# Stores moved to ScalarE's queue, four staging tiles and smaller weight-sum stores in a two-half SwiGLU feed-forward

## The chip, the cores and the metric

The kernel runs on one core of one Trainium2 chip. The metric is device microseconds of one execution; the time of a kernel is the median of its runs. Engines are named as in the profile: PE (TensorE; PEld is its weight load), DVE (VectorE), ACT (ScalarE), POOL (GpSimd) and SP (SyncE, which here only issues DMAs). ACT, too, has a DMA queue of its own.

## The reference

A transformer block in fp32 on x of 2048 x 576: a modulation from `c`, a layer norm, attention with a compressive memory in 4 segments and 32 heads of 18, a residual, a second layer norm, and a SwiGLU feed-forward with a hidden size of 4608, with a residual. The change touches the feed-forward alone:

```python
def _B_ref(x, w_gate, w_up, w_down):
    g = _silu(x @ w_gate)
    u = x @ w_up
    return (g * u) @ w_down
...
h = _layernorm(x, axis=-1) * (1 + cb) + sb
x = x + gb * _B_ref(h, B_w_gate, B_w_up, B_w_down)
```

## The kernel before, in words

The first 640 us are modulation, projections and attention. Then the feed-forward runs in two halves of 1024 tokens (`t` = 0 and 1), each a loop over 18 pairs `p` of hidden blocks (256 hidden columns). In each pair the gate product (z = 0) and the up product (z = 1) are formed as a 2 x 2 x 2 block product with seven products instead of eight (a Strassen scheme): a tile `O` of seven operands for the weights, a tile `y` of seven operands for the activations, and fixed sums of the products. A pair is therefore 14 steps `k`, one product each: seven matmuls of 512 columns (L1148), since each fp32 operand is split in a high and a low part: ACT casts the high part (`wh`, L1112), DVE subtracts for the low part (`wl`, L1113). `order` gives the sequence of the products. Casts run six steps ahead in the first half, five in the second.

`O` has 7 slots of [3][128] fp32 a partition: two full blocks of 128 contraction rows and a third block that holds the remainder of 32 rows four times. Four slots are loaded from HBM (`load_o`, L1081, 768 KB); three more and a replacement of the fourth are sums of them, made by POOL in four instructions (`sum_o`, L1103), so four slots (0, 4, 5, 6) hold sums. Only `prep_r` reads the third block; it makes the tile `wr` of the remainder (ACT cast L1097, DVE subtract L1098). In the first half the sums are stored to HBM (`store_o`: two DMAs to `oD`, 192 and 576 KB, all three blocks of the four slots), as is `wr` (`store_r` to `rD`, 336 KB), and the sums of the down-projection weights (`wdD`, 1008 KB, L1465). The second half reads all three back (L1083 to L1085, L1094, L1122) and does no sums. `O` has two buffers, so the load of the next tile waits until the last `wl` of the tile two back is done.

All of this is an order written out by hand (`manual_schedule`). What a step issues stands in the loop from L1412 on. The steps of a first-half pair that matter here, before the change:

- step 0 and 1: `mul_d`, two multiplies on POOL of the down-projection weights `RW` by a modulation row; steps 2, 3, 8 and 7: `sum_d`, their sums on POOL; steps 4, 5, 6 and 10: `prep_d`, ACT casts of the slots of `RW` and DVE subtractions.
- step 1: `load_o` of the next pair's z = 0, then the stores of this pair's z = 1 sums and z = 0 `wr`. Step 7: the store of the z = 1 `wr`. Step 8: `load_o` of the next pair's z = 1. Step 9: the store of `RW`, and the cast of the next pair's z = 0 remainder. Step 11: the store of the next pair's z = 0 sums. Step 12: the load of the next `RW`, a single buffer.
- steps 4 to 11: the down product of the previous pair, `plain`, 12 matmuls of 288 columns in each (L1288), added to `acc` by DVE (L1292).
- steps 1 to 10, in pairs after the first: one stage each of the generator `prep2`, which makes the second half's activation operands. It first normalizes five row blocks (load `ha` L1017, statistics L1024, store L1030), then for six pieces loads `xb` (L1040, L1043), transposes it on PE (L1048), evacuates it into `ha` (L1050) and makes seven operands. Each operand takes two stages: an ACT cast into a staging tile `st` (L1004), then a DVE subtraction (L1008 or L1011) and a store to `yD` (L1009 or L1012).

All these loads and stores are issued by SP, one after the other: a DMA whose wait isn't over holds up all that stand behind it. `st` has one buffer, so a cast into it waits until the store before has landed. The last first-half pair loads the seven operands `y` of the second half as their buffers come free (`load_y`), and with them the first `O` tiles and `wr` of the second half.

Of the kernel before, what the change touches and what calls it, by code (L numbers as in the profile page):

```python
# [7 lines left out]
F32 = mybir.dt.float32  # L8
F32R = mybir.dt.float32r
BF16 = mybir.dt.bfloat16  # L10
AF = mybir.ActivationFunctionType
ALU = mybir.AluOpType
# [3 lines left out]
P = 128  # L16
# [8 lines left out]
NF = FF // P  # L25
# [45 lines left out]
def f32(ap):  # L71
    return ap.bitcast(F32)
# [3 lines left out]
def block(ctx: ExitStack, tc: tile.TileContext, x, wqk, wv, wo, beta, wgu, wd, c, w_mod, out):  # L76
    nc = tc.nc
# [28 lines left out]
    dr = pool(ctx, "dr", space=DRAM)  # L106
# [42 lines left out]
    xD = [dr.tile([P, 4, D], F32, tag=f"xD{s}", name=f"xD{s}") for s in range(NSEG)]  # L149

    wdD = [dr.tile([P, 7, 288], F32, tag=f"wd{p}", name=f"wd{p}") for p in range(NF // 2)]
    oD = [[dr.tile([P, 4, 3, P], F32, tag=f"oD{p}_{z}", name=f"oD{p}_{z}") for z in range(2)] for p in range(NF // 2)]

    rD = [[dr.tile([96, 7, P], F32, tag=f"rD{p}_{z}", name=f"rD{p}_{z}") for z in range(2)] for p in range(NF // 2)]

# [92 lines left out]
    with ExitStack() as p1:  # L248
# [78 lines left out]
        with ExitStack() as p0:  # L327
# [27 lines left out]
            for p in (1, 0):  # L355
                for k in range(6):
                    for h in range(2):
                        r = 64 * (1 - p) + 32 * h
                        w = wm[p, k // 2][:, k % 2, 256:576] if h else wm[p, k // 2][:, k % 2, 0:256]
# [147 lines left out]
        for s in range(NSEG):  # L507
# [13 lines left out]
            for t in QKORD:  # L521
                if s == 0 and t + 3 < 9:
                    load_qk(t + 3)
                f = proj(s, t)
# [134 lines left out]
    op = pool(p2r, "op", side="right")  # L659
# [235 lines left out]
    NPR = NF // 2  # L895
# [10 lines left out]
            return ZML if p == NPR - 1 else ZM  # L906
        return ZM1 if p else ZMB

    SLOT = {1: 1, 2: 2, 3: 6, 4: 3, 5: 4, 6: 5, 7: 0}
    ACT_OP = {1: 0, 2: 1, 3: 2, 4: 6, 5: 3, 6: 4, 7: 5}  # L910

    def t_prep():
# [83 lines left out]
    def prep2():  # L996
        ha = xp.tile([P, 2, L], F32, tag="xs", name="ha")
        xb = xp.tile([P, 4, 2, P], F32, tag="xs", name="xb")[:, :, 0]
        t3 = x2p.tile([P, 256], F32, tag="t3", name="t3")

        def opr(kb, hv, o, f):
            n = P if kb < 2 else 96
            st = x2p.tile([P, 2, 256], F32R, tag="st", name="st")
            nc.scalar.copy(st[:n, 0], f)  # L1004
            c = slice(256 * hv, 256 * hv + 256)
            yield
            if kb < 2:
                nc.vector.tensor_tensor(st[:, 1], f, f32(st[:, 0]), op=ALU.subtract)  # L1008
                nc.sync.dma_start(yD[o][:, kb:kb + 3:2, c], f32(st))  # L1009
            else:  # L1010
                nc.vector.tensor_tensor(st[64:96, 0], f[64:96], f32(st[64:96, 0]), op=ALU.subtract)  # L1011
                nc.sync.dma_start(yD[o][:96, 4, c], f32(st[:96, 0]))  # L1012
            yield

        xl = ha.rearrange("p a b -> p (a b)")[:, :D]
        for sn, i in ((2, 3), (3, 0), (3, 1), (3, 2), (3, 3)):
            nc.sync.dma_start(xl, xD[sn][:, i, :])  # L1017
            for _ in range(3):
                yield
            st = x2p.tile([P, 2, 6], F32, tag="st3", name="st3")  # L1020
            mv = x2p.tile([P, 2], F32, tag="mv", name="mv")
            rs = x2p.tile([P, 1], F32, tag="rs", name="rs")
            for h in range(2):
                nc.vector.bn_stats(st[:, h, :], xl[:, 288 * h:288 * h + 288])  # L1024
            nc.vector.bn_aggr(mv, st)
            nc.vector.tensor_scalar(rs, mv[:, 1:2], EPS, None, op0=ALU.add)
            nc.gpsimd.tensor_tensor(rs, rs, mhalf[:, :1], op=ALU.pow)
            yield
            nc.vector.tensor_scalar(xl, xl, mv[:, 0:1], rs[:, 0:1], op0=ALU.subtract, op1=ALU.mult)
            nc.sync.dma_start(xhD[sn][:, i, :], xl)  # L1030
            yield
        for kb in range(3):
            n = P if kb < 2 else 96
            for hv in range(2):
                for kh in range(2):
                    c0 = 288 * kh + 128 * kb
                    for b in range(2):
                        src = xhD[2 + b][:, 2 * hv:2 * hv + 2, c0:c0 + min(P, 288 - 128 * kb)]
                        if kb < 2:
                            nc.sync.dma_start(xb[:, 2 * b:2 * b + 2, :], src)  # L1040
                        else:
                            for j in range(3):
                                nc.sync.dma_start(xb[:, 2 * b:2 * b + 2, 32 * j:32 * j + 32], src)  # L1043
                    for _ in range(3):
                        yield
                    pt = ps.tile([P, 4, P], F32, tag="M", name="pt", bufs=4)
                    for i in range(4):
                        nc.tensor.transpose(pt[:n, i, :], xb[:, i, :n], ident)  # L1048
                    c = 3 * kh + kb
                    nc.scalar.activation(ha[:n, kh], pt[:n].rearrange("p a b -> p (a b)"), AF.Identity,  # L1050
                                         scale=colm[:n, c, 0:1], bias=colm[:n, c, 1:2])
                    yield
                h00, h10, h01, h11 = [ha[:n, k, 256 * b:256 * b + 256] for k in range(2) for b in range(2)]
                nc.gpsimd.tensor_tensor(t3[:n], h11, h10, op=ALU.subtract)
                yield from opr(kb, hv, 0, h00)
                nc.gpsimd.tensor_tensor(h10, h10, h00, op=ALU.subtract)
                yield from opr(kb, hv, 5, t3[:n])
                yield from opr(kb, hv, 2, h11)
                yield from opr(kb, hv, 3, h10)
                nc.gpsimd.tensor_tensor(h11, h11, h10, op=ALU.subtract)  # L1060
                yield from opr(kb, hv, 1, h01)
                yield from opr(kb, hv, 4, h11)
                nc.gpsimd.tensor_tensor(h01, h01, h11, op=ALU.subtract)
                yield
                yield from opr(kb, hv, 6, h01)
# [5 lines left out]
    O, W, R, RW, DP = {}, {}, {}, {}, {}  # L1071
# [6 lines left out]
    def load_o(t, p, z):  # L1078
        O[p, z] = o = opl.tile([P, 7, 3, P], F32, tag="O", name="O", bufs=2)
        if t == 0:  # L1080
            nc.sync.dma_start(o[:, 0:4], wgu[p, z])  # L1081
        else:
            nc.sync.dma_start(o[:, 1:4], wgu[p, z][:, 1:4])  # L1083
            nc.sync.dma_start(o[:, 0], oD[p][z][:, 0])
            nc.sync.dma_start(o[:, 4:7], oD[p][z][:, 1:4])  # L1085

    def store_o(p, z):
        nc.sync.dma_start(oD[p][z][:, 0], O[p, z][:, 0])
        nc.sync.dma_start(oD[p][z][:, 1:4], O[p, z][:, 4:7])

    def prep_r(t, p, z):
        R[z] = r = wrp.tile([P, 7, P], F32R, tag="wr", name="wr")
# [6 lines left out]

    def sum_o(p, z, j):  # L1100
        o = O[p, z]
        d, a, b, op = ((4, 0, 3, ALU.add), (5, 4, 1, ALU.subtract), (0, 1, 0, ALU.subtract), (6, 2, 5, ALU.subtract))[j]
        nc.gpsimd.tensor_tensor(o[:, d], o[:, a], o[:, b], op=op)  # L1103

    def store_r(p, z):
        nc.sync.dma_start(rD[p][z], f32(R[z][0:96]))

    def prep_w(p, z, m):
        o = O[p, z][:, SLOT[m], 0:2]
# [14 lines left out]
    def mul_d(p, f):  # L1124
        v = RW[p][:, 2 * f:2 * f + 2].rearrange("p a b -> p (a b)")
        nc.gpsimd.tensor_tensor(v, v, gbB, op=ALU.mult)

    def sum_d(p, j):
        r = RW[p]
        d, a, b = ((4, 1, 0), (5, 3, 4), (6, 2, 5), (1, 3, 1))[j]  # L1130
        nc.gpsimd.tensor_tensor(r[:, d], r[:, a], r[:, b], op=ALU.subtract)
# [109 lines left out]
    NS = [7] * (NPR - 2) + [4] * 2  # L1241
# [65 lines left out]
    with tc.manual_schedule():  # L1307
# [51 lines left out]
        for i in range(4):  # L1359
            for h in range(2):  # L1360
                for c in range(WC):
# [8 lines left out]
                    if n in SS:  # L1370
                        j = SS.index(n)
# [22 lines left out]
        x2p = pool(p6, "x2p")  # L1394
# [17 lines left out]
        for p in range(NPR):  # L1412
# [4 lines left out]
            for k in range(14):  # L1417
                z, m = order(0, p)[k]
# [18 lines left out]
                else:  # L1437
# [5 lines left out]
                        prep_r(0, p, 1)  # L1443
                    elif k == 9:
                        prep_r(0, nx, 0)
                if k < 2:
                    mul_d(p, k)
                elif k in (2, 3, 8, 7) and p < NPR - 2:
                    sum_d(p, (2, 3, 8, 7).index(k))
                if not end and 4 <= k < 8:  # L1450
                    sum_o(nx, 0, k - 4)
                elif not end and 9 <= k < 13:
# [1 line left out]
                if k in (4, 5, 6, 10):  # L1454
                    j = (4, 5, 6, 10).index(k)
                    prep_d(p, (j // 2, j % 2), j)
                if k == 0 and p == 0:
                    store_o(p, 0)
                elif k == 1:
                    store_o(p, 1)  # L1460
                    store_r(p, 0)
                elif k == 7:
                    store_r(p, 1)
                elif k == 9:
                    nc.sync.dma_start(wdD[p][:, :NS[p]], RW[p][:, :NS[p]])  # L1465
                elif k == 11 and not end:
                    store_o(nx, 0)
                elif k == 12 and not end:
                    load_d(0, nx)
# [12 lines left out]
        for p in range(NPR):  # L1482
# [5 lines left out]
            for k in range(14):  # L1488
                z, m = order(1, p)[k]
# [72 lines left out]
def _pairs(*ws):  # L1562
    import numpy as np

    n = ws[0].shape[1] // 256
    w = np.stack(ws, axis=0).reshape(len(ws), 2, 288, n, 2, P)
    w = w.transpose(3, 0, 4, 1, 2, 5)
    r = w[..., 256:, :]
    w = np.concatenate([w[..., :256, :], r, r, r, r], axis=-2)
    w = w.reshape(n, len(ws), 2, 2, 3, P, P).transpose(0, 1, 5, 2, 3, 4, 6)  # L1570
    return np.stack([w[:, :, :, 1, 0], w[:, :, :, 0, 0], w[:, :, :, 0, 1], w[:, :, :, 1, 1]], axis=3)


# [29 lines left out]
```

## Time and profile before

| | before |
|---|---|
| median of 3 runs (lowest to highest) | 2037.23 us (2030.49 to 2041.49) |
| profiled execution | 2030.05 us, span 2028.3 us |
| mean granted TensorE clock | 0.978 |
| busy: PE, PEld | 1911.1 us, 1581.1 us |
| busy: DVE, ACT, POOL | 1592.9, 890.5, 580.1 us |
| DMA of SP's queue (q1) | 314.71 MB |
| DMA of ACT's queue (q10) | 5.93 MB |

The span is the time from the first to the last instruction of the profiled execution. Busy time leaves out instructions that only issue a DMA or wait on a semaphore. Matmuls are pipelined: 405 ns is listed for one of 512 columns, but seven of them in a row take 1.62 us in the chain. The first half of the feed-forward goes from about 645 to 1390 us, the second from there to the end. "A <- B" in a list of waits means that A's engine sat idle until B was done.

### The profile page before, as it was taken

Reading aid. Unit: us, or ns where it says so; the run is one execution under the profiler, and the core shown is the slowest. Engines: PE = TensorE matmul, PEld = TensorE weight load, DVE = VectorE, ACT = ScalarE, POOL = GpSimd, SP = SyncE. Lnnn points to the kernel's source line nnn. Section 1 sums busy time; section 2 is a strip of 40 time slices with the busy share of each in tenths; the row PEclk is TensorE's granted clock in tenths of the full one; section 3 lists DMA queues with packets and bytes.
Section 4 is the critical chain, followed back from the end, with each engine's and each line's share of the span. In section 5 each row is a group of like instructions: output and inputs, shape, how many; then the busy total and the mean of one; then the engine's idle time right before and its main releaser. Section 6 shows DMA issues by size and latency. Waiting matters only on the chain.

```text
span 2028.3 us, 30981 instructions
## 1 busy us (share of the span) xinstructions
PE 1911.1 (94%) x10927; PEld 1581.1 (78%) x10927; DVE 1592.9 (79%) x3411; ACT 890.5 (44%) x1928; POOL 580.1 (29%) x772
## 2 busy tenths in 40 slices
PE   7999989999997899989989998888999999999998
PEld 5888846776766687878878877777888888888888
DVE  7564268787868889888878898785888888888886
ACT  2222267777665333343334333233444445454442
POOL 5222246455445534444434443320000000000000
PEclk9999999999998999999999999899999999999999
DMA  7676654545425654545445544458543434343441
GB/s 228 239 240 222 221 174 124 149 133 154 119 85 152 226 180 164 167 142 190 136 146 172 190 128 135 140 170 271 164 145 121 143 123 143 123 143 123 143 140 51
DMA packets 147050, 322.61 MB, mean 159 GB/s; under 512 B 26256, under 2 KB 61456, under 8 KB 145424
## 3 DMA queue, kind: packets, MB, share of 16 engines
q1 hardware_dynamic: 144640, 314.71, 48.1%
q10 hardware_dynamic: 2256, 5.93, 0.8%
q8 instruction: 86, 1.41, 0.3%
q14 instruction: 68, 0.56, 0.1%
HBM read 201.80 MB, written 118.75 MB: 158 GB/s over the span
## 4 chain that ended last, share of the span: by engine, by line
PE 69%; DVE 17%; DMA 8%; issue 2%; ACT 2%; SPq 1%; POOL 1%; ACTq 0%; DVEq 0%; POOLq 0%
PE A L1148 12%; PE pd L1271 9%; PE pd L1288 9%; PE M L1148 7%; PE C L1148 6%; PE pp L102 4%; PE s L590 4%; PE av L610 4%; PE s L188 4%; DVE wl L1113 3%; PE B L1148 3%; PE pw L708 2%; DMA yD<-st 2%; PE pv L102 2%; DVE sg L1171 2%
## 5 line engine op out<-in xcount | busy, mean ns | idle before, releaser
L1148 PE MATMUL M<-y,wh 128*128 128x512 f32 x1008 | 366.6, 405 | 23.0 <-DVE cu L1170 14.1
L193 DVE CUSTOM_DVE_ANT_0 junk<-s,tri 128x256 bf16<-128x256 f32 (+3 forms) x512 | 228.7, 486 | 76.1 <-PE s L188 68.5
L1113 DVE TENSOR_TENSOR wl<-O,wh 128x256 fp32r<-128x256 f32 x504 | 262.5, 522 | 2.3 <-ACT wh L1112 1.4
L1148 PEld LDWEIGHTS M<-y,wh 128*128 128x128 f32 x1008 | 195.5, 194 | 74.0 <-issue 19.4
L1231 ACT CAST ah<-sg 128x512 fp32r<-128x512 f32 x192 | 118.7, 618 | 277.2 <-DVE sg L1171 214.7
L1103 POOL TENSOR_TENSOR O<-O 128x384 f32<-128x384 f32 x144 | 160.9, 1131 | 251.1 <-DMA O<-in_wgu_dram 90.3
L593 ACT ACTIVATE Pt<-s 128x512 f32<-128x512 f32 (+1 forms) x352 | 186.6, 559 | 86.8 <-PE s L590 72.8
L1288 PE MATMUL pd<-dh,ah 128*128 128x288 f32 x640 | 194.1, 303 | 29.1 <-DVE acc L1292 29.1
L1148 PE MATMUL A<-y,wh 128*128 128x512 f32 x576 | 203.5, 394 | 0.7 <-ACT cu L1176 0.7
L1148 PE MATMUL M<-y,wl 128*128 128x512 f32 x504 | 202.6, 402 | 0.0
L1112 ACT CAST wh<-O 128x256 fp32r<-128x256 f32 x504 | 199.1, 402 | 3.9 <-DMA O<-in_wgu_dram 2.3
L1288 PE MATMUL pd<-dh,al 128*128 128x288 f32 x640 | 193.2, 302 | 1.4 <-DVE al L1232 1.4
L1288 PE MATMUL pd<-dl,ah 128*128 128x288 f32 x640 | 193.1, 302 | 0.0
L1276 DVE TENSOR_TENSOR acc<-acc,pd 128x576 f32<-128x576 f32 x216 | 159.0, 748 | 24.2 <-PE pd L1271 22.5
L1232 DVE TENSOR_TENSOR al<-sg,ah 128x512 fp32r<-128x512 f32 x192 | 144.4, 752 | 21.0 <-ACT ah L1231 21.0
L1292 DVE TENSOR_TENSOR acc<-acc,pd 128x576 f32<-128x576 f32 x156 | 116.7, 748 | 54.7 <-PE pd L1288 53.5
L590 PE MATMUL s<-qs,ks 110*128 110x512 f32 (+2 forms) x384 | 150.6, 409 | 4.9 <-DMA qs<-mD 3.4
L1288 PEld LDWEIGHTS pd<-dh,ah 128*128 128x128 f32 x640 | 124.6, 195 | 39.0 <-DVE acc L1292 33.0
L1163 ACT ACTIVATE sg<-sg 128x512 f32<-128x512 f32 x109 | 68.9, 632 | 178.2 <-DVE sg L1162 178.2
L188 PE MATMUL s<-ks,qs 108*128 108x256 f32 (+3 forms) x512 | 141.6, 328 | 3.8 <-DMA ks<-kD 2.1
L1271 PE MATMUL pd<-dh,ah 128*128 128x288 f32 x448 | 132.8, 296 | 0.0
L1271 PE MATMUL pd<-dh,al 128*128 128x288 f32 x448 | 132.6, 296 | 0.0
(367 smaller groups left out, 4623.0 us busy)
## 6 DMA issues: line engine op xcount, KB each, us to landing
O<-in_wgu_dram SPq DMA_DIRECT2D x36, 768.0 KB
oD<-O SPq DMA_DIRECT2D x36, 576.0 KB
O<-in_wgu_dram SPq DMA_DIRECT2D x36, 576.0 KB
O<-oD SPq DMA_DIRECT2D x36, 576.0 KB
ks<-kD SPq DMA_DIRECT2D x68, 216.0 KB
qs<-qD SPq DMA_DIRECT2D x68, 216.0 KB
rD<-wr SPq DMA_DIRECT2D x36, 336.0 KB
wr<-rD SPq DMA_DIRECT2D x36, 336.0 KB
```

The costliest lines, as they stand in the source:

```text
L188: nc.tensor.matmul(bank[:, n * (h - h0):n * (h - h0) + n], lhsT=qst[b][0:108, h, 128 * i:128 * i + 128], rhs=kst[b][0:108, h // 2, 0:n], s ...
L193: nc.vector.tensor_tensor_reduce(junk[:, :n], bank[:, n * (h - h0):n * (h - h0) + n], tri[:, L - n:], 1.0, -3e38, op0=ALU.add, op1=ALU.max ...
L590: nc.tensor.matmul(bank[:, n * (g - h):n * (g - h + w)].rearrange("p (a b) -> p a b", a=w), lhsT=kst[u % NB][0:110, g // 2, 128 * j:128 * ...
L593: nc.scalar.activation(pt[:, h:h + per, :n], bank[:, :n * per].rearrange("p (a b) -> p a b", a=per), AF.Exp, scale=SCALE)
L1103: nc.gpsimd.tensor_tensor(o[:, d], o[:, a], o[:, b], op=op)
L1112: nc.scalar.copy(wh, o)
L1113: later.append(lambda: nc.vector.tensor_tensor(wl, o, f32(wh), op=ALU.subtract))
L1148: nc.tensor.matmul(bank, lhsT=a, rhs=b, start=(first and n == 0), stop=(n == 6), skip_group_check=not first)
L1232: later.append(lambda: nc.vector.tensor_tensor(al, src, f32(ah), op=ALU.subtract))
L1271: nc.tensor.matmul(pd[:, i, :288], lhsT=a[:, tk], rhs=w, start=(k == 0), stop=(k == 2))
L1276: nc.vector.tensor_tensor(o, o, pd[:, :, :288], op=ALU.add)
L1288: nc.tensor.matmul(pd[:, i, :288], lhsT=a[:, tk], rhs=w, start=(k == 0), stop=(k == 5))
```

## The change

- `store_o`, `store_r` and the store of `RW` are issued by ACT's queue instead of SP's. The store of `RW` moves from step 9 to step 10.
- `st` gets four buffers instead of one.
- The four slots that hold sums become 3 to 6, next to each other (the host lays the blocks out in another order, and `SLOT` and `sum_o` follow it), and only their first two blocks are stored, in one DMA of 512 KB. The second half loads two blocks of all seven slots, in two DMAs (384 and 512 KB).
- `mul_d` moves from steps 0 and 1 to 1 and 2, the first two `sum_d` from steps 2 and 3 to 3 and 4.

```diff
-    oD = [[dr.tile([P, 4, 3, P], F32, tag=f"oD{p}_{z}", name=f"oD{p}_{z}") for z in range(2)] for p in range(NF // 2)]
+    oD = [[dr.tile([P, 4, 2, P], F32, tag=f"oD{p}_{z}", name=f"oD{p}_{z}") for z in range(2)] for p in range(NF // 2)]
...
-    SLOT = {1: 1, 2: 2, 3: 6, 4: 3, 5: 4, 6: 5, 7: 0}
+    SLOT = {1: 0, 2: 1, 3: 6, 4: 2, 5: 4, 6: 5, 7: 3}
...
-            st = x2p.tile([P, 2, 256], F32R, tag="st", name="st")
+            st = x2p.tile([P, 2, 256], F32R, tag="st", name="st", bufs=4)
...
-            nc.sync.dma_start(o[:, 1:4], wgu[p, z][:, 1:4])
-            nc.sync.dma_start(o[:, 0], oD[p][z][:, 0])
-            nc.sync.dma_start(o[:, 4:7], oD[p][z][:, 1:4])
+            nc.sync.dma_start(o[:, 0:3, 0:2], wgu[p, z][:, 0:3, 0:2])
+            nc.sync.dma_start(o[:, 3:7, 0:2], oD[p][z])
...
     def store_o(p, z):
-        nc.sync.dma_start(oD[p][z][:, 0], O[p, z][:, 0])
-        nc.sync.dma_start(oD[p][z][:, 1:4], O[p, z][:, 4:7])
+        nc.scalar.dma_start(oD[p][z], O[p, z][:, 3:7, 0:2])
...
-        d, a, b, op = ((4, 0, 3, ALU.add), (5, 4, 1, ALU.subtract), (0, 1, 0, ALU.subtract), (6, 2, 5, ALU.subtract))[j]
+        d, a, b, op = ((4, 3, 2, ALU.add), (5, 4, 0, ALU.subtract), (3, 0, 3, ALU.subtract), (6, 1, 5, ALU.subtract))[j]
...
     def store_r(p, z):
-        nc.sync.dma_start(rD[p][z], f32(R[z][0:96]))
+        nc.scalar.dma_start(rD[p][z], f32(R[z][0:96]))
...
-                if k < 2:
-                    mul_d(p, k)
-                elif k in (2, 3, 8, 7) and p < NPR - 2:
-                    sum_d(p, (2, 3, 8, 7).index(k))
+                if k in (1, 2):
+                    mul_d(p, k - 1)
+                elif k in (3, 4, 8, 7) and p < NPR - 2:
+                    sum_d(p, (3, 4, 8, 7).index(k))
...
-                elif k == 9:
-                    nc.sync.dma_start(wdD[p][:, :NS[p]], RW[p][:, :NS[p]])
+                elif k == 10:
+                    nc.scalar.dma_start(wdD[p][:, :NS[p]], RW[p][:, :NS[p]])
```

More of the change, by code (lines that the diff above doesn't have):

```diff
@@ L1570, in _pairs @@
     w = w.reshape(n, len(ws), 2, 2, 3, P, P).transpose(0, 1, 5, 2, 3, 4, 6)
-    return np.stack([w[:, :, :, 1, 0], w[:, :, :, 0, 0], w[:, :, :, 0, 1], w[:, :, :, 1, 1]], axis=3)
+    return np.stack([w[:, :, :, 0, 0], w[:, :, :, 0, 1], w[:, :, :, 1, 1], w[:, :, :, 1, 0]], axis=3)
 def kernel(**inputs):
```

## The prediction

> **What bounds the kernel now.** I read the page's summary first, then the chain, then stretches of the span, then the waits of the first half of the feed-forward (640 to 1370 us), and last the timeline around one stall. The chain by engine says that the end is set mostly by TensorE:
>
> ```profile
> PE 69%; DVE 17%; DMA 8%; issue 2%; ACT 2%; SPq 1%; POOL 1%; ACTq 0%; DVEq 0%; POOLq 0%
> ```
>
> Next, busy time by stretch (us, then PE, PEld, DVE, ACT, POOL busy with counts, granted clock, DMA share, GB/s). The first two stretches are each one pair of the first half, cut at the ACT cast of the remainder tile that step 9 issues (L1097); the third is a pair of the second half.
>
> ```profile
> 877.98:915.68 37.70, 36.54 (x204) 32.09 (x203) 33.69 (x52) 15.00 (x35) 16.95 (x15) 1.00 0.50 166
> 996.09:1041.26 45.17, 39.18 (x201) 33.93 (x200) 35.16 (x56) 15.73 (x37) 18.51 (x17) 0.92 0.43 142
> ...
> 1460.00:1494.00 34.00, 34.00 (x183) 29.57 (x182) 28.86 (x55) 16.33 (x38) 0.00 (x0) 1.00 0.40 132
> ```
>
> The second half is PE alone: 34.00 of 34.00 us. Nothing that shortens its loads can show there. In the first half the same work takes 37.7 or 45.2 us, and the longer pair has idle PE and a granted clock of 0.92. The waits (total us, times, longest) tell what differs:
>
> ```profile
> ACT st L1004 <- DMA yD<-st: 70.7, 16, 7.7
> ...
> PE pd L1288 <- DVE acc L1292: 29.1, 9, 5.2
> ...
> DVE st L1008 <- ACT st L1004: 24.6, 5, 6.9
> ...
> DVE st L1024 <- DMA ha<-xD: 11.1, 3, 3.9
> ...
> PE pt L1048 <- DMA xb<-xh: 9.7, 3, 5.8
> ```
>
> And the timeline shows one of the 16 (start, duration, engine, line; in brackets the idle time before):
>
> ```profile
> 1016.02 0.33 SPq L1081 DMA_DIRECT2D O<-in_wgu_dram  x1
> 1016.46 0.37 SPq L1088 DMA_DIRECT2D oD<-O  x1
> ...
> 1016.87 0.43 SPq L1089 DMA_DIRECT2D oD<-O  x1
> ...
> 1017.34 0.45 SPq L1106 DMA_DIRECT2D rD<-wr  x1
> ...
> 1017.84 8.63 SPq L1009 DMA_DIRECT2D yD<-st  x2
> ...
> 1025.21 0.41 ACT L1004 CAST st<-t 128x256 fp32r<-128x256 f32 x1 [7.66 <-DMA yD<-st]
> ...
> 1025.64 0.43 DVE L1008 TENSOR_TENSOR st<-t,st 128x256 fp32r<-128x256 f32 x1 [6.85 <-ACT st L1004]
> ...
> 1029.31 0.61 PE L1288 MATMUL pd<-dh,ah 128*128 128x288 f32 x1 [5.17 <-DVE acc L1292]
> ```
>
> At step 1 of a pair SP issues a 768 KB load, two stores of together 768 KB and one of 336 KB, and behind them the small store of the staging tile `st`. There is one `st`, so the next cast into it stops ACT until that store lands, 7.4 us after its issue; DVE then lacks ACT, and PE lacks DVE.
>
> **The change, part by part.**
>
> *Four `st` tiles.* The cast now waits for the store four operands back. An operand takes two steps of about 2.7 us, so four are some 21 us, against 7.4 us for the slow store seen: the waits on `st` go. What that is worth I work out in two ways. Directly: the PE gaps of the row "PE pd <- DVE acc" that follow a `st` wait are 5.21, 1.93, 5.17, 1.23, 3.11 and 5.05 = 21.7 us (its other three, 7.4 us, follow a `ha` wait). Behind five of them PE ran at half the granted clock for 4.1, 3.4, 5.6, 3.4 and 4.7 us, which loses half of 21.2 = 10.6. Together 32 us. By pairs: between step-9 casts the seven periods with a `st` wait of over 3 us and no PE wait on `xb` are 44.5, 40.5, 45.2, 40.4, 40.8, 44.4 and 41.5 = 297.3 us; the calm ones are 36.2, 37.7 and 36.0. Seven times 37.7 leaves 33.4, seven times their mean 36.6 leaves 41. I take 33, because a calm period may have lived on work done ahead, and keep 41 as an end. What is late next in such a pair: DVE, 33.7 us busy of 37.7, and PE, 36.5, so nothing below 36.5 is to be had. That floor is why not the whole 70.7 us comes back.
>
> *Bulk stores from ACT's queue: what it takes off SP's.* Behind the same bulk stand the `ha` loads (three pairs, periods 37.8, 41.4, 41.7: 7.8 us over 37.7 in all) and the `xb` loads (39.9, 40.1 and 46.5: 13.4 over). Together 21 us are at stake. On SP the stores in front of such a load shrink from 1104 KB to none, but the 768 KB load in front stays, and 848 KB of stores still move at that time. ACT reaches step 1 two to three us before SP gets free (SP waits there for the last `wl`), so the stores start earlier. No row shows two busy queues, so the ends are 0 and 21; I take 8, a bit over a third, as 1104 of 1872 KB in front leave the queue but not the engines.
>
> The row to weigh is the page's DMA share, 0.43 to 0.53 in these pairs: the engines have room on average, but not within the burst. The Trainium skill (DMA: Bandwidth & Descriptors, "Issuing engines are not separate DMA queues") says that DMAs issued by several engines run on the same 16 DMA engines and interleave, and that issuing from more of them saves only the issue time. By that rule this term would be 0 and the sum 32 instead of 40; it is the first rival below.
>
> *What it costs ACT.* Per pair ACT now issues two `oD` stores (one DMA each, where SP had two), two `rD` and one `wd`. On SP an `oD` issue took 0.42 us, an `rD` 0.45 and a `wd` 0.42; ACT's own issues took 0.31 to 0.34. That is 5 x 0.31 = 1.6 to 2.2 us a pair, 18 pairs: 28 to 39 us if it all lay on the path. It lies beside ACT's waits for DVE: in 640 to 1370 us ACT waited 203.9 us for `sg` ahead of `ah` and 104.4 ahead of the activation, 17 us a pair, in the very steps 1, 7, 10 and 11. I charge 3 us in all, and keep 0 and 39 as ends. Queued behind a store that has to wait are the weight casts, which run six steps ahead of PE, and the activations, which DVE and PE need within a step or two.
>
> *The new waits on ACT.* An `oD` store waits for the POOL sums, which SP did before. In the trace the fourth sum of the first tile ended 2.9 to 15.7 us before ACT's step-11 cast, that of the second 7.3 to 15.0 us before ACT's step-1 cast (1004.3 against 1015.6 in the pair shown); the last `sum_d` 1.3 to 10.7 us before step 10. So ACT finds them done: 0. The `wd` store leaves some 3 us later than SP's did (step 10 instead of 9), and the next down-projection load must wait for it, as it did 8 times already (25 us in all on SP). What hides it: the multiplies ended about 18 us before the first cast that reads them at step 4 in the pair shown (1010.8 against 1029.2), still some 10 in a calm one. 1 us for this; without the cover 3 us a pair, 48.
>
> *`mul_d` and `sum_d` a step later, the slots renumbered.* POOL runs steps ahead of ACT here and starts the multiplies when their data land; the same four sums in the same order. 0; within a us a pair either way.
>
> *Fewer bytes.* Stores: 36 x 256 KB less, under a DMA share of 0.5: 0. Second-half loads: 1344 to 896 KB per tile, under a PE that is busy all the time: 0. In the change between the halves (1350 to 1395 us, DMA share 0.96, 315 GB/s) two such loads stand in front of the `wr` load for which PE waits 4.69 us, followed by 5.5 us at half clock. 0.92 MB less at 315 GB/s is 2.9 us: I take 3, ends 0 and 4.7 + 2.7 = 7.
>
> **Sum:** -33 - 8 + 3 + 1 - 3 = -40 us. The profiled execution took 2030.05 us (span 2028.3 and 1.75 around it), so it would take 1990. The runs shown have a median of 2037.23, 7 us more; nothing in the sum depends on that difference, so against the median I forecast 2037 - 40 = **1997 us**.
>
> **Rivals.**
> - *The move to ACT's queue frees nothing* (the engines are shared, `ha` and `xb` still wait): -33 - 3 + 4 = -32, 2005 us. For it: the 768 KB load stays in front. Against: the stores leave earlier, and there are fewer bytes. 0.20.
> - *Everything calms*: pairs at 36.6 (-41), half of the 21 us, 5 at the change of halves: -57, less 3 of cost, 1983 us. 0.10.
> - *The issues land on ACT's path in full*: -33 - 8 - 3 + 39 + 1 = -4, 2033 us. Against: 17 us of ACT waits a pair. 0.06.
> - *Four tiles are not enough or the cast waits for something else*, so that the `st` wait is only renamed: -7, 2030 us. Against: 21 us of cover for stores of 7.4. 0.02.
> - *Slower: a store stops ACT.* Place: the `oD` store at step 1, behind POOL's fourth sum. 70.7 us of ACT waits cost 33 now, 0.47 a us. To lose 40 and 10 more takes 106 us over 34 such stores, 3.1 us each, so POOL would have to end 10 us later than now; at 5 us each it is 80 us, 2077 us. Decided by whether the tile's load lands that late beside the stores. Against: that slack of 7.3 us at least. 0.05.
>
> The forecast keeps 0.57. Its own range is 1985 to 2010. With both neighbours and part of the costs of issue the range is 1975 to 2020; its low end is between the second rival and all terms at their far ends (-41 - 21 - 7 + 1 = -68, 1969), its high end the forecast with half of the issue cost on the path. Outside lie the third, fourth and fifth rival. Within 0.5% (10 us, about what a measurement of this kernel can tell from no change) lie the third and fourth: 0.08; slower 0.05; faster 0.87.
>
> **What would show it.** The row "ACT st <- DMA yD" is gone or under 5 us; DVE's wait for ACT ahead of `st` too; the gaps "PE pd <- DVE acc" fall from 29 to under 10 us; periods between step-9 casts gather at 37 to 38 us; ACT's queue carries some 48 MB more, with no ACT wait for POOL at its stores; a pair of the second half stays at 34.0. The forecast is wrong if ACT shows waits of several us at its stores, if the `ha` and `xb` waits grow, or if calm pairs come out above 39 us.

## The result, and the profile after

The changed kernel takes 1985.26 us (median of 4 runs, 1981.84 to 1991.21) against 2038.07 (2030.49 to 2041.49): a ratio of 0.9749, 95% interval 0.9712 to 0.9786. That is 12 us below the forecast of 1997 us, at the low edge of the forecast's own range (1985 to 2010) and inside the whole range (1975 to 2020). Of the terms, the bytes were put too low, and how the other queue helps was told wrongly, as the experiments show.

The profiled execution of the changed kernel has a span of 1989.4 us, the slowest of its four runs. Its first summary line answers to the one of before: SP's queue is off the chain, DMA falls from 8 to 5%, DVE rises from 17 to 22%.

```profile
PE 65%; DVE 22%; DMA 5%; issue 3%; ACT 3%; POOL 1%; ACTq 0%; SPq 0%; DVEq 0%; POOLq 0%
```

The stretches, in the columns shown before: a usual pair of the first half, the two long ones, and a pair of the second half.

```profile
869.50:907.10 37.60, 35.51 (x197) 30.86 (x196) 33.93 (x52) 15.10 (x35) 17.09 (x15) 1.00 0.47 160
944.70:986.30 41.60, 38.14 (x192) 32.43 (x191) 33.53 (x53) 14.58 (x34) 17.52 (x15) 0.92 0.46 151
1214.20:1257.70 43.50, 37.73 (x190) 32.12 (x189) 33.94 (x53) 15.23 (x34) 16.13 (x14) 0.92 0.43 137
1400.00:1434.00 34.00, 34.00 (x183) 29.61 (x182) 28.60 (x55) 16.45 (x38) 0.00 (x0) 1.00 0.32 102
```

The second half is untouched at 34.0 us, though its DMA share fell from 0.40 to 0.32. In the first half the periods between step-9 casts are 34.9, 37.5, 38.3, 36.7, 38.2, 37.6, 37.6, 41.6, 37.6, 37.3, 37.2, 38.1, 38.4, 39.3, 43.6 and 38.7 us, against 36.0 to 46.5 before. The waits of 640 to 1380 us (`cu` is a sum by DVE that reads a finished product out of its bank, which PE needs again; `wh` and `wl` are the parts of a weight operand):

```profile
PE M L1146 <- DVE cu L1168: 14.8, 13, 2.0
...
DVE wl L1111 <- ACT wh L1110: 13.8, 15, 1.6
...
PE pt L1048 <- DMA xb<-xh: 6.6, 3, 3.9
...
PE pd L1286 <- DVE acc L1290: 2.3, 5, 0.6
...
DVE st L1024 <- DMA ha<-xD: 1.1, 3, 0.5
```

ACT's wait for `yD<-st` (70.7 us) is gone, and the PE gaps behind `acc` fell from 29.1 to 2.3. The second row is new: before, DVE waited 1.4 us in all for a weight cast. The timeline of step 1 shows what it is (an ACTq row is an issue on ACT's own queue):

```profile
1005.11 0.33 SPq L1081 DMA_DIRECT2D O<-in_wgu_dram  x1
...
1005.72 0.63 ACT L1161 ACTIVATE sg<-sg 128x512 f32<-128x512 f32 x1 [0.71 <-DVE sg L1160]
1005.78 0.57 ACTq L1087 DMA_DIRECT2D oD<-O  x1
...
1006.05 3.23 SPq L1009 DMA_DIRECT2D yD<-st  x2
...
1006.40 0.64 ACTq L1104 DMA_DIRECT2D rD<-wr  x1
1007.08 0.41 ACT L1110 CAST wh<-O 128x256 fp32r<-128x256 f32 x1 [0.72 <-issue]
1007.39 0.40 ACT L1004 CAST st<-t 128x256 fp32r<-128x256 f32 x1
...
1007.51 0.43 DVE L1111 TENSOR_TENSOR wl<-O,wh 128x256 fp32r<-128x256 f32 x1 [0.56 <-ACT wh L1110]
```

The small store now follows the load directly on SP (1006.05, 0.94 us behind it; it stood 1.82 us behind it before), and the cast into the next `st` (1007.39) waits for nothing. But ACT's two issues hold up a weight cast, and DVE waits for it.

**Where the time went, by place.** Both programs issue the same matmuls in the same order, so the n-th matmul marks the same work. I cut at three of them: the body of the first half (4200th to 7350th), the change of halves (to the 7650th) and the second half (to the 10800th).

| us | before | after | difference |
|---|---|---|---|
| up to the 4050th (code not touched) | 640.7 | 648.3 | +7.6 |
| 4050th to 4200th | 45.9 | 45.3 | -0.6 |
| body of the first half | 658.6 | 617.0 | -41.6 |
| change of halves | 69.4 | 65.2 | -4.2 |
| second half | 589.1 | 589.0 | -0.1 |

The feed-forward gains 46.5 us. The +7.6 arises in the first 360 us, in code that neither kernel changes, and other kernels' profiled executions reach that matmul at 641.9 to 648.3 us: single executions differ there, so I compare by these stretches. Each stretch comes from one profiled execution of a kernel. The medians differ by 52.8 us; with the interval, 44 to 59 us, that agrees with the 46.5.

### The profile page after: what moved, and what is told of

The parts are those of the page before. It is cut to its first block, busy times and chain, and to the rows that moved or that the text cites. A ratio compares the mean times of both kernels' runs of the same rounds, so it can differ in the third digit from the quotient of the medians.

```text
span 1989.4 us, 30854 instructions
## 1 busy us (share of the span) xinstructions
PE 1904.3 (96%) x10927; PEld 1573.1 (79%) x10927; DVE 1598.7 (80%) x3411; ACT 894.3 (45%) x1928; POOL 583.4 (29%) x772
## 4 chain that ended last, share of the span: by engine, by line
PE 65%; DVE 22%; DMA 5%; issue 3%; ACT 3%; POOL 1%; ACTq 0%; SPq 0%; DVEq 0%; POOLq 0%
PE A L1146 12%; PE pd L1269 9%; PE C L1146 6%; PE pd L1286 6%; PE M L1146 5%; DVE wl L1111 4%; PE s L590 4%; PE av L610 4%; PE pp L102 4%; PE s L188 4%; PE B L1146 3%; PE pv L102 3%; PE pw L708 2%; DVE sg L1169 2%; DVE acc L1290 2%
## 5 line engine op out<-in xcount | busy, mean ns | idle before, releaser
L1146 PE MATMUL M<-y,wh 128*128 128x512 f32 x1008 | 364.0, 402 | 22.1 <-DVE cu L1168 14.8
L1111 DVE TENSOR_TENSOR wl<-O,wh 128x256 fp32r<-128x256 f32 x504 | 269.4, 535 | 14.4 <-ACT wh L1110 13.8
L1101 POOL TENSOR_TENSOR O<-O 128x384 f32<-128x384 f32 x144 | 164.8, 1158 | 229.3 <-DMA O<-in_wgu_dram 120.7
L1286 PE MATMUL pd<-dh,ah 128*128 128x288 f32 x640 | 190.0, 297 | 2.3 <-DVE acc L1290 2.3
L1286 PE MATMUL pd<-dl,ah 128*128 128x288 f32 x640 | 189.3, 296 | 0.0
L1269 PE MATMUL pd<-dh,ah 128*128 128x288 f32 x448 | 132.8, 296 | 0.0
L1269 PE MATMUL pd<-dl,ah 128*128 128x288 f32 x448 | 132.5, 296 | 0.0
```

What stands on the lines that cost most here:

```text
L1111: later.append(lambda: nc.vector.tensor_tensor(wl, o, f32(wh), op=ALU.subtract))
L1146: nc.tensor.matmul(bank, lhsT=a, rhs=b, start=(first and n == 0), stop=(n == 6), skip_group_check=not first)
L1269: nc.tensor.matmul(pd[:, i, :288], lhsT=a[:, tk], rhs=w, start=(k == 0), stop=(k == 2))
L1286: nc.tensor.matmul(pd[:, i, :288], lhsT=a[:, tk], rhs=w, start=(k == 0), stop=(k == 5))
```

## The experiments

All ratios are to the kernel before, timed on the same chip, with 95% intervals. "Body" and "change" are the two stretches of the table above. Theory A is the prediction's: three terms, `st` the largest. The main rival is that the bulk stores in SP's queue are the whole cause.

| kernel | ratio | body, us | change, us | ACT waits for `st` | `ha` | `xb` |
|---|---|---|---|---|---|---|
| before | 1 | 658.6 | 69.4 | 70.7 | 11.1 | 9.7 |
| e1: four `st` | 0.9847 (0.9828 to 0.9866) | 630.3 | 70.8 | none | 11.0 | 9.3 |
| e2: queue | 0.9922 (0.9907 to 0.9938) | 644.7 | 65.7 | 55.0 | none | 9.8 |
| e3: bytes | 0.9925 (0.9912 to 0.9939) | 647.5 | 65.6 | 62.4 | 8.5 | 7.1 |
| e4: after, one `st` | 0.9855 (0.9836 to 0.9874) | 632.1 | 65.8 | 55.3 | 0.6 | 6.9 |
| e5: after, stores on SP | 0.9805 (0.9791 to 0.9818) | 621.7 | 65.8 | none | 8.2 | 6.3 |
| after | 0.9749 (0.9712 to 0.9786) | 617.0 | 65.2 | none | 1.1 | 6.6 |

**e1: only the four tiles.**

```diff
-            st = x2p.tile([P, 2, 256], F32R, tag="st", name="st")
+            st = x2p.tile([P, 2, 256], F32R, tag="st", name="st", bufs=4)
```

> Only the four st tiles, all else as before. Theory A (the st wait is the main term, worth 33 us by the calm pairs, and does not depend on the queue): ratio to before 0.984 (about 2005 us), the row ACT st <- DMA yD under 5 us, the gaps PE pd <- DVE acc from 29 to some 8 us (those behind the ha loads stay), the PE wait for wr of 4.7 us at the change of halves stays. Theory B (the bulk stores in SP's queue are the cause, and more tiles only move the wait to ha, xb or the next weight load): ratio above 0.992.

0.9847, as theory A has it. In the waits the row for `st` is gone, and of the gaps behind `acc` those that follow `ha` remain:

```profile
DVE st L1024 <- DMA ha<-xD: 11.0, 3, 3.7
...
PE pt L1048 <- DMA xb<-xh: 9.3, 3, 4.7
...
PE pd L1288 <- DVE acc L1292: 7.2, 6, 3.7
```

So the depth of `st` is worth 28 us in the body with all stores still in SP's queue, and neither `ha` nor `xb` got worse.

**e2: only the queue.** The stores as before (two for `oD`), on ACT's queue, `wd` at step 10.

```diff
-        nc.sync.dma_start(oD[p][z][:, 0], O[p, z][:, 0])
-        nc.sync.dma_start(oD[p][z][:, 1:4], O[p, z][:, 4:7])
+        nc.scalar.dma_start(oD[p][z][:, 0], O[p, z][:, 0])
+        nc.scalar.dma_start(oD[p][z][:, 1:4], O[p, z][:, 4:7])
...
+        nc.scalar.dma_start(rD[p][z], f32(R[z][0:96]))
...
+                    nc.scalar.dma_start(wdD[p][:, :NS[p]], RW[p][:, :NS[p]])
```

> Only the bulk stores on ACT's queue (oD as two DMAs of all three blocks, rD, and wd at step 10), one st tile. Theory A: the small store still stands behind the 768 KB load, the st wait falls by some 40 percent (70.7 to about 42 us); 13 us for that, 8 for ha and xb, less 4 for ACT's issues: ratio 0.991 to 0.993 (about 2021 us). Theory B: the st wait falls below 20 us and the ratio is 0.985 or less. Theory C (ACT's issues cost what they take, 28 to 39 us): ratio 1.00 or more.

0.9922: theory A's size; the rival's 0.985 and the full cost of the issues are both excluded.

```profile
ACT st L1004 <- DMA yD<-st: 55.0, 17, 5.6
...
PE pd L1288 <- DVE acc L1292: 19.1, 10, 4.5
...
DVE wl L1113 <- ACT wh L1112: 18.8, 16, 1.8
```

The `st` wait shrank by 22% (I expected 40): with the 768 KB load in front of it and the stores beside it, the small store still lands late. The `ha` wait went, the `xb` wait did not, and the wait of DVE for the weight cast appeared, 18.8 us.

The timelines show what the move gave. SP no longer issues three stores between the load and what follows it: the small store stood 1.82 us behind the load and now stands 0.93, `ha` and the late `xb` loads stood 1.8 us behind it and now 0.4. Once issued, they gain less. Where the small store stands closest behind the load, the cast that waits for it starts 5.8 to 7.1 us after its issue, against 7.2 to 7.4 before; DVE takes up `ha` 6.2 to 6.4 us after its issue, with almost no wait, against 7.1 to 7.5; and the `xb` load with the longest wait takes 8.7 us instead of 7.2, which eats up its earlier start. So a large part of this term is time that SP spent issuing, 1.4 us, in front of a transfer that an engine waits for. Of the 14.8 us by which the listed periods shrink, the three `ha` pairs give 9.6.

**e3: only the bytes.** The new slots, two-block stores in one DMA and two-block loads; stores on SP, one `st`, steps as before.

```diff
-        nc.sync.dma_start(oD[p][z][:, 0], O[p, z][:, 0])
-        nc.sync.dma_start(oD[p][z][:, 1:4], O[p, z][:, 4:7])
+        nc.sync.dma_start(oD[p][z], O[p, z][:, 3:7, 0:2])
```

> Only the renumbered slots and the two-block stores and loads; stores on SP, one st tile, steps as before. Theory A: 3 us at the change of halves and some 5 from a burst that is 256 of 1872 KB smaller: ratio 0.996 (about 2030 us), the second half's pairs stay at 34.0 us. If the smaller packets (1 KB instead of 1.5 and 4.5 KB) cost more than the bytes save, the ratio is 1.00 or above.

0.9925, about twice the gain expected: 3.8 us at the change of halves, as forecast (though the queue alone gives 3.7 there in e2), but 11.1 in the body, where the prediction had put nothing. The waits behind the burst are each a little shorter:

```profile
ACT st L1004 <- DMA yD<-st: 62.4, 16, 6.9
...
DVE st L1024 <- DMA ha<-xD: 8.5, 3, 2.9
```

The longest `st` wait went from 7.7 to 6.9 us, the longest `ha` wait from 3.9 to 2.9. At 315 GB/s, the rate of the crowded change of halves, 256 KB are 0.83 us, an estimate of what the burst lost. One DMA instead of two also lets SP go on sooner, but that is 0.13 us only (the small store 1.68 us behind the load instead of 1.82). Beside other edits the same step is worth as much: 8.6 us of body with four tiles (e1 to e5), 12.6 with the stores on ACT's queue (e2 to e4).

**e4: the changed kernel with one `st` again.**

```diff
-            st = x2p.tile([P, 2, 256], F32R, tag="st", name="st", bufs=4)
+            st = x2p.tile([P, 2, 256], F32R, tag="st", name="st")
```

> The changed kernel with one st tile again. Theory A (the terms add): the changed kernel's 0.975 plus 0.016, ratio 0.990. Theory B (the queue move alone would have emptied the wait): ratio below 0.981, st waits below 20 us. If the terms overlap, something between, and the st wait then tells how much of it the queue had removed.

0.9855, between: queue and bytes together give 26.5 us in the body, and four tiles then add 15.1 instead of 28.3. The terms overlap: the `st` wait is already down to 55.3 us, in 17 stalls of at most 5.1 us instead of 16 of at most 7.7. The overlap is with the queue, since with the stores on SP four tiles still add 25.8 us (e3 to e5).

**e5: the changed kernel with its stores on SP, `wd` at step 9.**

```diff
-        nc.scalar.dma_start(oD[p][z], O[p, z][:, 3:7, 0:2])
+        nc.sync.dma_start(oD[p][z], O[p, z][:, 3:7, 0:2])
...
-        nc.scalar.dma_start(rD[p][z], f32(R[z][0:96]))
+        nc.sync.dma_start(rD[p][z], f32(R[z][0:96]))
...
-                elif k == 10:
-                    nc.scalar.dma_start(wdD[p][:, :NS[p]], RW[p][:, :NS[p]])
+                elif k == 9:
+                    nc.sync.dma_start(wdD[p][:, :NS[p]], RW[p][:, :NS[p]])
```

> The changed kernel with the stores on SP's queue again (wd at step 9): four st tiles and the two-block stores remain. Alone, st gave 28.3 us in the body of the first half, the queue 13.9 and the bytes 11.1, together 41.6. Theory A (each takes bytes or waits out of the same burst, so what the queue still gives is what ha and xb lose there, 6 to 8 us): ratio 0.978 to 0.980. If with four tiles the queue gives nothing: 0.975. If it gives its full 14 us: 0.982.

0.9805. With four tiles and fewer bytes the queue still gives 4.7 us of body in the two profiled executions, a little less than expected; by the ratios it is 11 us, with both intervals some 4 to 19, so its size is known only roughly. In the periods the three `ha` pairs lose 7.6 us (the `ha` wait falls from 8.2 to 1.1) and the other thirteen together grow by 3.5, which may be what ACT's issues cost; 3.0 of the 3.5 lie in one pair with an `xb` wait.

**e7: two tiles in the changed kernel.**

```diff
-            st = x2p.tile([P, 2, 256], F32R, tag="st", name="st", bufs=4)
+            st = x2p.tile([P, 2, 256], F32R, tag="st", name="st", bufs=2)
```

> The changed kernel with two st tiles. Theory A: a cast then waits for the store two operands back, four steps or about 10 us, and the slowest store with the bulk on the other queue lands in 5.1 us: no st wait over 1 us, ratio 0.975 as with four. If the depth of four is used (several small stores held up together behind one load): st waits of 10 us or more in total, ratio 0.979 or more.

0.9762 (0.9747 to 0.9777), body 619.0, and 1.8 us of `st` waits: by the ratio two tiles can't be told from four. (The 5.1 us of the expectation is the longest `st` wait in e4, not a time to landing.)

**e6: `mul_d` and `sum_d` a step earlier, as before the change.**

```diff
-                if k in (1, 2):
-                    mul_d(p, k - 1)
-                elif k in (3, 4, 8, 7) and p < NPR - 2:
-                    sum_d(p, (3, 4, 8, 7).index(k))
+                if k < 2:
+                    mul_d(p, k)
+                elif k in (2, 3, 8, 7) and p < NPR - 2:
+                    sum_d(p, (2, 3, 8, 7).index(k))
```

> The changed kernel with the multiplies and first sums of the down-projection weights a step earlier again (steps 0 and 1, 2 and 3). Theory A: POOL runs ahead and starts them when their data land, so nothing moves: ratio 0.974 to 0.977. Rival (the later multiplies contend less with DVE where DVE is short): ratio 0.979 or more.

0.9769 (0.9754 to 0.9784), body 618.0: not to be told from the changed kernel, as forecast.

**e8: the step-1 load last.** In the changed kernel, `load_o(0, nx, 0)` is issued at the end of step 1.

```diff
-                    if k == 1:
-                        load_o(0, nx, 0)
...
                     next(g2, None)
+                if not end and k == 1:
+                    load_o(0, nx, 0)
```

> The changed kernel with the 768 KB load of step 1 issued behind that step's stage of the operand preparation, so that small transfers of the step no longer stand behind it. Theory A (what is left of the ha and xb waits is that load in front): the two long pairs of 41.6 and 43.6 us fall below 40, ratio 0.970 to 0.972. Rival: the load now waits behind a small store that waits for DVE, leaves 1 to 4 us later, and POOL's sums with it; slack of 7 us covers that, else ACT waits at its stores and the ratio is 0.977 or more.

0.9735 (0.9722 to 0.9749), body 610.4. The ratio can't be told from the changed kernel's (0.9712 to 0.9786); the body of the profiled execution is 6.6 us shorter. Of the two long pairs one fell (43.6 to 37.9 us), the other not (41.6 to 40.9).

**e9: the multiplies on DVE.**

```diff
-        nc.gpsimd.tensor_tensor(v, v, gbB, op=ALU.mult)
+        nc.vector.tensor_tensor(v, v, gbB, op=ALU.mult)
```

> The changed kernel with the two multiplies of the down-projection weights on DVE instead of POOL, same steps. While POOL multiplies (1.85 us each) a DVE subtraction takes 1.66 instead of 0.42 us and one of 512 columns 1.9 instead of 0.68, 2.4 us a pair. On DVE the two cost about 0.75 us each. Theory A (the contention is what leaves the PE gaps behind cu of 14.8 us): 1 us a pair less, ratio 0.967 to 0.972. Rival (steps 12 to 3 have no down product and are bound by DVE's own work, so that 1.5 us more of it cost in full, and the contention was partly idle time): ratio 0.978 or more.

0.9691 (0.9677 to 0.9704), body 599.9: 17 us less than the changed kernel. Before the change POOL and DVE met like this:

```profile
1007.54 3.27 POOL L1126 TENSOR_TENSOR dr__12226<-dr__12226,gbB 128x576 f32<-128x576 f32 x2 [3.22 <-DMA dr__12226<-in_wd_dram]
...
1009.44 1.65 DVE L1113 TENSOR_TENSOR wl<-O,wh 128x256 fp32r<-128x256 f32 x1
1011.01 1.29 DVE L1232 TENSOR_TENSOR al<-sg,ah 128x512 fp32r<-128x512 f32 x1
```

The subtraction of 0.42 us takes 1.65 beside POOL. On DVE a multiply takes 0.75 us, and PE's gaps behind `cu` are nearly gone:

```profile
PE M L1146 <- DVE cu L1168: 3.8, 5, 2.0
...
DVE wl L1111 <- ACT wh L1110: 0.2, 1, 0.2
```

The second row shows a rival that this run doesn't exclude: DVE's wait for the weight cast, 13.8 us in the changed kernel, is gone too, although ACT's issues are as long as before. DVE now multiplies in the time in which it stood still behind them. How much of the 17 us is contention and how much is this idle time put to use stays open.

**e11: twice the issues on ACT, the same bytes.** Each of the stores is split in two halves of the partitions.

```diff
+        for h in (slice(0, 64), slice(64, 128)):
+            nc.scalar.dma_start(oD[p][z][h], O[p, z][h, 3:7, 0:2])
...
+        for h in (slice(0, 48), slice(48, 96)):
+            nc.scalar.dma_start(rD[p][z][h], f32(R[z][h]))
...
+                    for h in (slice(0, 64), slice(64, 128)):
+                        nc.scalar.dma_start(wdD[p][h, :NS[p]], RW[p][h, :NS[p]])
```

> The changed kernel with each store on ACT's queue split in two halves of the partitions: the same bytes, 180 issues instead of 90, which took ACT 44 us in all. Theory A (the issues lie beside ACT's waits for DVE): ACT issues for some 30 us more, the ratio is within 0.003 of the changed kernel's 0.975. Rival (ACT's issues are on the path in full or by half): ratio 0.982 to 0.990.

1.0017 (1.0005 to 1.0029): the whole gain is lost. Theory A falls here, and the time lies outside the rival's range as well. ACT's issues take 128.6 us instead of 44.4, far more than double. The timeline of one step 1, on ACT:

```profile
861.45 0.63 ACTq L1088 DMA_DIRECT2D oD<-O  x1
862.17 3.53 ACTq L1106 DMA_DIRECT2D rD<-wr  x2
865.75 0.41 ACT L1112 CAST wh<-O 128x256 fp32r<-128x256 f32 x1 [4.34 <-DMA oD<-O]
```

The casts stand still until the fourth issue is through, and DVE waits for them:

```profile
DVE wl L1113 <- ACT wh L1112: 58.3, 15, 4.9
```

The body is 52 us longer than the changed kernel's, for 84 us more of issue. The halves also change how each DMA is laid out and how many are in flight, and all stores were split, not those of step 1 alone, so this run doesn't tell the issue's own time from a queue that pushes back. It shows that DMAs on ACT's queue can hold up the casts and reach the path.

**e12: the stores of step 1 at steps 4 and 5.** The changed kernel otherwise.

```diff
-                elif k == 1:
+                elif k == 4:
                     store_o(p, 1)
+                elif k == 5:
                     store_r(p, 0)
```

> The changed kernel with the two stores of step 1 moved to steps 4 and 5, still on ACT's queue. There the pair is bound by PE, and no 768 KB load starts. In the changed kernel DVE waits 13.8 us in 15 pairs for a weight cast that ACT makes only after the two issues of step 1. Theory A (those waits are the cost of ACT's issues, and they lie in the steps that DVE bounds): the row DVE wl <- ACT wh falls below 3 us, most pairs lose half a us or more, ratio 0.968 to 0.971. Rival (the waits are taken up by slack later in the pair): ratio 0.973 to 0.977, with the row gone all the same.

0.9681 (0.9666 to 0.9695), body 601.3: 15.7 us less than the changed kernel. DVE's wait for the cast is back to 1.4 us, and there is no wait on `ha` or `xb` at all; the two long pairs fell from 41.6 and 43.6 to 37.0 and 39.7 us. In the periods that is 8.5 us of 14.7; the other 14 pairs lost 0.44 us each. I take that to be the issues' part, but the edit also moves the bytes of the two stores away from the load, and no run separates the two.

**e10: e8 and e9 together.** The two edits above, for instance:

```diff
-        nc.gpsimd.tensor_tensor(v, v, gbB, op=ALU.mult)
+        nc.vector.tensor_tensor(v, v, gbB, op=ALU.mult)
...
+                if not end and k == 1:
+                    load_o(0, nx, 0)
```

> The changed kernel with both edits that gained: the step-1 load behind the operand stage (ratio 0.9735) and the multiplies on DVE (0.9691). Theory A (one frees small transfers, the other DVE): the gains add, ratio 0.966 to 0.968. Rival (with DVE's order now holding the multiplies, a later load moves POOL's sums and eats the gain): 0.969 or more.

0.9642 (0.9625 to 0.9658), 1964.89 us, body 593.9: somewhat better than expected, and the fastest kernel of this study. e12's edit on top of it wasn't run; here DVE's wait for the weight cast is already down to 0.2 us, so part of e12's gain is probably taken already.

## Why the prediction was right, and where its steps were off

The mechanism of the main term was right: one staging tile behind a burst in SP's queue stopped ACT, then DVE, then PE; the change took the stall away, most pairs gathered at 37 to 38 us, the second half didn't move. Forecast -40 us, measured -46.5 in the feed-forward. That the sum came so close is in part luck: the prediction left out a term of 9 to 13 us and added others that overlap by about as much. Term by term:

- **Four `st` tiles, -33.** Alone 28.3 us of body and a ratio of 0.9847 (31 us): right. In the changed kernel they are the 15.1 us between e4 and after; the prediction added terms that overlap. Alone the three give 28.3 + 13.9 + 11.1 = 53.3 us of body, together 41.6; the overlap is between the tiles and the queue (e4).
- **Bulk stores from ACT's queue, -8, less 3 for the issues and 1 for `wd`.** Net 4.7 us of body beside the other edits (e5 to after), against 4 forecast; by the ratios some 4 to 19, so the sum is not contradicted, and no more. How it came was told wrongly: the stores do not leave two to three us before SP's load, but 0.6 to 0.7 us behind it in 16 of 17 pairs (1005.78 against 1005.11 in the pair shown), later than the 0.4 us at which SP sent the first of them. ACT's issues stand behind an activation that waits for DVE, and the trace of before had it already at 1016.62, 0.60 us behind the load. What was won is SP's issue time ahead of `ha` (e2); the `xb` wait stayed. No run tests the 1 us for `wd` by itself.
- **The issues on ACT, 3 us.** The size isn't refuted (3.5 us between e5 and after; some 6 in e12, with what moving the bytes gives); the issues themselves took 44.4 us where 28 to 39 were expected, and their cover was misread. ACT's 17 us of idle time a pair are waits for DVE, and an issue hides beside them only where DVE isn't waiting for ACT in turn. In step 1 it is: 13.8 us of new DVE waits. All 36 `oD` issues took 0.52 to 0.59 us and no row of ACT's waits names POOL at a store, so the slower rival never came near. SP did wait longer for `oD` stores to land ahead of its 768 KB load (71.0 us against 20.2) and POOL for that load (120.7 against 90.3), without reaching ACT. But e11 shows that twice as many DMAs on ACT's queue undo the change, at a price of one issue that the prediction did not have.
- **Fewer bytes, 0 in the first half.** This is the step that failed most: 11.1 us alone (e3), 8.6 and 12.6 beside other edits. The prediction argued from a mean DMA share of 0.5 that bytes there cost nothing; but the stores stand in the burst that the small transfers wait behind. Within it the share is 0.73 (1016.0 to 1025.2 us of before), and with 256 KB less the cast behind the slow small store starts some 8.2 us after the load instead of 9.1. At the change of halves -3 was forecast and 3.8 to 4.2 measured; but e2, with all bytes left in place, gains 3.7 there too, so that the bytes are its cause isn't shown (the 0.96 and 315 GB/s of its working belong to 1352 to 1392 us).
- **`mul_d` a step later, 0:** right (e6).

The first rival was "the move to ACT's queue frees nothing", with the rule of the Trainium skill (DMA: Bandwidth & Descriptors, "Issuing engines are not separate DMA queues") beside it: the engines are shared, and only issue time is saved. The `st` wait of 55.0 us in e2 agrees with that, and so does the `xb` wait, 9.8 us against 9.7. The prediction's mistake was to read the rule as a term of 0. The issue time saved was SP's 1.4 us ahead of `ha` and `xb`, and because DVE waited for `ha`, e2 as a whole gained 13.9 us of body. `ha` was there at least 2 us sooner after the load, so the issue time is not all of it.

What stays open: what shortens the change of halves in e2; how much of e11's 52 us is issue time and how much a queue that pushes back; how much of e9's gain is contention; and how e12's splits between issues and bytes. Why `xb` waits as long in e2 as before, the runs suggest: its wait goes with the bytes beside it, on whichever queue they are. It is 9.3 to 9.8 us with the large stores (before, e1, e2), 4.9 to 7.7 with the smaller ones (e3 to e7, e9 and after), and none once the stores leave step 1 (e12).

## What to carry to other kernels

Look for the small transfer that stands behind a burst: there the bytes beside it cost, however low the mean DMA share, and so does each DMA that its queue issues ahead of it; a second buffer for the small tile is the cheapest cure. Moving bulk DMAs to a computing engine's queue saves that issue time, but each issue is an instruction of that engine: put it at steps where nobody waits for that engine, and never several in a row. Where idle time is offered as cover, ask who waits for whom in just that step.

## What the runs showed of the hardware that I had not expected

- A DMA issue cost no more on ACT than on SP here, and its time goes with the DMA and with what was issued just before it: the `oD` store of 512 KB took 0.53 us on ACT (after) and 0.53 on SP (e3), the `wd` store 0.34 and 0.42 (medians). `rD` took 0.31 us by itself on ACT and 0.58 to 1.60 right behind an `oD`; in e11 two halves of `rD` behind two of `oD` took 3.53. On ACT no cast starts meanwhile.
- A 128x256 subtraction on DVE took 1.65 us instead of 0.42 while POOL multiplied 128x576 in SBUF. The pair of multiplies cost POOL 3.3 us and DVE itself 1.5; moving them to the busier engine made the kernel 0.6% faster.
- Between 640 and 1400 us of the kernel before, each of the nine gaps on PE of 3 us or more had the granted clock at half at its end or just behind it, for 3.4 or 6.8 us (once 10.2); so had some of the gaps of 1.8 to 2.9 us and none of the shorter ones. By the prediction's estimate this turned 21.7 us of gaps behind `st` waits into 32.
